# Sliding-window attention and mixture of experts on one core: how a block's values reach the partitions

## The chip, the core and the metric

The kernel runs on one core of a Trainium2 chip. The metric is the device time of one execution in microseconds (us), lower is better. The kernel before takes 676.07 us, the median of three runs (673.82 to 677.14).

## The reference

Eight batches of eight heads with 576 positions of 64 numbers go through masked attention; heads 0 to 3 see the 32 latest keys, heads 4 to 7 see every fourth of the 128 latest. The attention's output, one row of 512 per token (4608 tokens), is then routed over eight experts with a capacity of 576 tokens each, and every expert is a two-layer network.

```python
mask_plain = (rel >= 0) & (rel < window)                                  # window = 32
mask_dil = (rel >= 0) & (rel < window * dilation) & (rel % dilation == 0) # dilation = 4
scores = np.where(masks[None, :, :, :], scores, -1000000000.0)
attn = np.exp(scores - np.max(scores, axis=-1, keepdims=True))
attn = attn / (np.sum(attn, axis=-1, keepdims=True) + 1e-09)
out = np.matmul(attn, v)
...
for e in range(E):
    mask = assigned == e
    out[mask] = np.maximum(x[mask] @ w1[e], 0.0) @ w2[e]
```

## The kernel before, in words

The kernel has two stages: attention (`attention`, L260 to L772), which writes its rows to a scratch tensor `xd` in device memory, and after it the search for the routing and the experts (`moe`). The change touches attention alone.

**Units.** Attention works through 8 batches. A batch has two kinds of heads: kind 0 the plain window, kind 1 the dilated one, whose sequence is put in an order in which it is a plain window of 32 too. A kind of a batch has two units of two heads each, so there are 32 units. For a unit PE makes the masked scores in two forms (`scan`, L498 and L502, for the maxima; `scores`, L509 and L514), ACT takes the exponentials into `E` (L468), PE multiplies them by the values (`values`, L526, tile `px`), DVE divides (L534 to L536, tile `xs`), PE turns the result for the gate (L585), and SP stores `xs` to `xd` (L545): two stores per batch for kind 0 and eight for kind 1.

**The values in SBUF.** `VT[kind][slot]` (tile `v` in the profile) has 128 partitions and nine columns, one for each 64 keys of a sequence; a column holds four heads of 65 numbers (64 and a one). There are two slots per kind, used by even and odd batches. Queries are taken 32 at a time and see 64 keys: even groups of 32 queries see the last 32 keys of the column before and the first 32 of their own, odd groups the first and the last 32 of their own. A column therefore holds, from partition 0 up: 32 keys of the column before, its own first 32, its first 32 again, and its last 32. So each half of a block stands in SBUF twice. The load (`load_v`, L292 to L295) brings all 64 keys to partitions 64 to 127, and copies within SBUF (`shift_v`, L297 to L303) make the other two quarters: L301 moves partitions 96 to 127 to partitions 0 to 31 of the next column, L303 moves partitions 64 to 95 to 32 to 63.

**`load_values`** (L400 to L412) does this once per kind and batch. It issues two loads on SP, columns 0 to 4 and 5 to 8 (325 and 260 KB; rows of 5200 and 4160 bytes). In the first batch DVE and ACT make the copies, in pieces of columns 0 to 4 and 5 to 8. From the second on POOL makes all of them, in pieces of 2, 3, 2 and 2 columns for each of the two quarters, so eight copies per kind and batch, 112 in all. `values` (L526) waits for all loads and copies of its kind and batch (`ready["V", kind, b]`).

**What sets the order.** Nobody writes the order of attention's instructions by hand: each step is an `Op` with an engine, an assumed cost, the steps it depends on and a bonus, and `Schedule.run` (L188) replays them against these costs, takes at each turn the most urgent step that can start, and so writes one order for each engine. A transfer on SP costs 475 ns of SP there, and its landing is assumed from its bytes (`sp`, L336 to L339). Engines then run their orders strictly in turn and wait on semaphores.

**What holds SP back.** `paced` (L321 to L334) adds a wait to a load or store: on a product of PE that the replay found done by then (`K.gate`), or, without one, on an earlier transfer, so that no more than 1.2 MB (`LIMIT`) are under way. The framework also gives every transfer one of eight semaphores in rotation (DMAHW0 to DMAHW7 below). The next transfer that uses a semaphore waits until the one that had it has landed. So no more than eight transfers from SP are under way.

Of the kernel before, what the change touches and what calls it, by code (L numbers as in the profile page):

```python
# [20 lines left out]
B, H, S, D = 8, 8, 576, 64  # L21
# [5 lines left out]
NB = S // 64  # L27
# [18 lines left out]
P_U, B_A, B_K, B_V, B_P, TOL_A, TOL_B, TOL_C, TOL_D = 4680, 15400, -5200, 14500, -105500, 650, 650, 300, 800  # L46
# [213 lines left out]
def attention(tc, ctx, C, load_const, T, xd, Lt, R):  # L260
    nc = tc.nc
# [7 lines left out]
    def op(eng, *a, **k):  # L269
        return K.op(eng, *a, tail=T_E[eng], **k)  # L270
# [6 lines left out]
    VT = [[pk.tile([128, NB, 4, D + 1], F32, name=f"v{x}{s}") for s in range(2)] for x in range(2)]  # L277
# [11 lines left out]
                  for n, k in (("pm", 2), ("pS", 2), ("px", 3)))  # L289
    act = lambda o, i: nc.scalar.activation(o, i, AF.Copy)  # L290

    def load_v(b, kind, c0, c1):  # L292
        w = 4 * (D + 1)
        return nc.sync.dma_start(VT[kind][b % 2][64:, c0:c1].rearrange("p c h d -> p (c h d)"),
                                 T["in_vp" if kind == 0 else "in_vd"][b][:, w * c0:w * c1])  # L295

    def shift_v(b, kind, part, f, c0, c1):  # L297
        t = VT[kind][b % 2].rearrange("p c h d -> p c (h d)")
        if part == 0:
            c1 = min(c1, NB - 1)  # L300
            f(t[:32, c0 + 1:c1 + 1], t[96:, c0:c1])  # L301
        else:
            f(t[32:64, c0:c1], t[64:96, c0:c1])  # L303

    users = {}

    def old(*key):
        u = users.get(key, [])
        users[key] = []
        return u  # L310
# [10 lines left out]
    def paced(fn, bytes_):  # L321

        def run():
            i, under_way = fn().ins, bytes_
            if K.gate:
                return after(i, K.gate, "transfers keep step with the products")
            for prev, z in reversed(flow):
                under_way += z
                if under_way > LIMIT:
                    after(i, prev.name, "few bytes under way")  # L330
                    break
            flow.append((i, bytes_))

        return run  # L334

    def sp(cost, fn, deps, bytes_, b, kind=0):  # L336
        first[0] -= 1e6
        return op("SP", 475 * cost, paced(fn, bytes_) if cost == 1 else fn, deps,
                  B_D - (4 * b + 2 * kind) * P_U if b else first[0], dma=bytes_ / D_R)  # L339
# [4 lines left out]
    ready = {}  # L344
# [55 lines left out]
    def load_values(b, kind):  # L400
        s = b % 2
        oldv = old("v", kind, s)
        ld = {c0: sp(1, lambda c0=c0, c1=c1: load_v(b, kind, c0, c1), oldv, 64 * (c1 - c0) * 4 * 65 * 4, b, kind)
              for c0, c1 in ((0, 5), (5, NB))}
        ready["V", kind, b] = list(ld.values())
        for part in range(2):
            eng = "POOL" if b else ("DVE", "ACT")[part]
            f = {"ACT": act, "DVE": nc.vector.tensor_copy, "POOL": nc.gpsimd.tensor_copy}[eng]
            for c0, c1 in ((0, 2), (2, 5), (5, 7), (7, 9)) if b else ((0, 5), (5, 9)):
                ready["V", kind, b].append(op(eng, {"ACT": 255, "DVE": 190, "POOL": 275}[eng] * (c1 - c0),  # L410
                                              lambda part=part, f=f, c0=c0, c1=c1: shift_v(b, kind, part, f, c0, c1),
                                              [ld[0 if c1 < 6 else 5], ready["b", kind, s]], -4 * b * P_U))  # L412

    load.q = None

# [331 lines left out]
    ready["r"] = sp(1, choosers, (), 131000, 0)  # L747
    load(0, 0, 1)
    load_values(0, 0)
    load(0, 1, 0)  # L750
    const(2)
    load(0, 1, 1)
    load_values(0, 1)
    const(3)

# [5 lines left out]
    for u in range(4 * B):  # L761
        b = u // 4
        if u % 4 == 0 and b:
            for kind in range(2):
                load(b, kind, 0)
                load(b, kind, 1)
                load_values(b, kind)
        Unit(u).build()
# [797 lines left out]
```

## Time and profile before

| what | value |
|---|---|
| median of three runs | 676.07 us (673.82 to 677.14) |
| profiled execution | 676.34 us |
| its span in the profile | 674.4 us |
| attention and its last products | 0 to about 182 us |
| search for the routing, first part | about 182 to 205 us |
| experts | about 205 us to the end |

The span is the stretch from the first to the last instruction in the trace; 1.94 us of the profiled execution's own time lie outside it. Times of the rows below count from the start of the span. PE is the matmul engine and PEld its weight loads, DVE, ACT and POOL are the other compute engines, and SPq rows are transfers as SP issues them.

### The profile page before, as it was taken

The numbers are of one execution on the slowest core, as the hardware profiler recorded it, in microseconds if no ns is written. First come the engines' busy times: TensorE is split into PE (matmuls) and PEld (weight loads), VectorE is DVE, ScalarE is ACT, GpSimd is POOL, SyncE is SP. The second block draws the span as 40 slices with busy tenths as digits, with TensorE's granted clock in tenths as the row PEclk, the third lists the DMA queues.
The fourth block names the chain that finished last, engine by engine and source line by source line (L and its number), as shares of the span: only waits on it lengthen the run. The fifth ranks groups of instructions, "written<-read, shape, count | busy, mean of one in ns | idle before, by whom it ended". The sixth has DMA issues, their size and how long they took to land.

```text
span 674.4 us, 19052 instructions
## 1 busy us (share of the span) xinstructions
PE 629.3 (93%) x7513; PEld 550.1 (82%) x7515; DVE 463.9 (69%) x1576; ACT 294.1 (44%) x644; POOL 208.3 (31%) x316
## 2 busy tenths in 40 slices
PE   7788998889857999999999999999999999999996
PEld 6777887778645988998899799889879978988985
DVE  6577878588677884689799588778959845623310
ACT  5655555355304825855345136334423525424211
POOL 6446754555004317524213112110420311311011
PEclk9999999899957999999999999999999999999999
DMA  8988879784205937967236116314502755213001
GB/s 240 261 255 218 246 219 263 208 227 147 73 1 178 225 70 200 275 142 250 93 97 209 48 56 209 113 55 141 181 33 58 262 181 163 66 37 103 1 24 47
DMA packets 51673, 99.09 MB, mean 147 GB/s; under 512 B 7168, under 2 KB 17152, under 8 KB 51584
## 3 DMA queue, kind: packets, MB, share of 16 engines
q1 hardware_dynamic: 42240, 72.71, 36.2%
q0 software_dynamic: 9344, 25.17, 13.8%
q8 instruction: 59, 0.97, 0.6%
q14 instruction: 30, 0.25, 0.1%
HBM read 72.69 MB, written 18.87 MB: 136 GB/s over the span
## 4 chain that ended last, share of the span: by engine, by line
PE 53%; DVE 19%; issue 14%; DMA 7%; POOL 4%; ACT 1%; POOLq 0%; SPq 0%; DVEq 0%; ACTq 0%
PE py L1432 15%; PE ph L1387 15%; PE px L526 4%; PE pS L514 4%; PE px L585 2%; POOL xg L1336 2%; DVE hb L1408 2%; PE ptx L1350 2%; DMA raw<-in_moe_w 1%; DVE xs L536 1%; DMA v<-in_vd 1%; PE pz L817 1%; POOL out L1458 1%; DVE G L831 1%; PE py L1435 1%
## 5 line engine op out<-in xcount | busy, mean ns | idle before, releaser
L1432 PE MATMUL py<-w2h,hb 128*128 128x512 f32 x512 | 170.4, 398 | 0.0
L1387 PE MATMUL ph<-xh,w1h 128*128 128x256 f32 (+1 forms) x512 | 138.3, 301 | 0.0
L1387 PE MATMUL ph<-xh,w1l 128*128 128x256 f32 (+1 forms) x512 | 136.4, 297 | 0.0
L1387 PE MATMUL ph<-xl,w1h 128*128 128x256 f32 (+1 forms) x512 | 136.2, 296 | 0.0
L1432 PEld LDWEIGHTS py<-w2h,hb 128*128 128x128 f32 x512 | 96.1, 188 | 19.1
L1212 ACT ACTIVATE hb<-ph 128x256 fp32r<-128x256 f32 (+2 forms) x192 | 59.6, 346 | 100.8 <-PE ph L1387 100.6
L1458 POOL DMA_INDIRECT out<-y,idx x40 | 41.8, 1045 | 199.1 <-ACT y L1212 143.5
L1432 PE MATMUL py<-w2l,hb 128*128 128x512 f32 x256 | 99.9, 390 | 0.0
L1387 PEld LDWEIGHTS ph<-xh,w1h 128*128 128x128 f32 x512 | 91.8, 189 | 0.6
L1387 PEld LDWEIGHTS ph<-xl,w1h 128*128 128x128 f32 x512 | 91.6, 190 | 0.0
L1387 PEld LDWEIGHTS ph<-xh,w1l 128*128 128x128 f32 x512 | 91.5, 190 | 0.0
L1408 DVE SCALAR_TENSOR_TENSOR hb<-ph,hb 128x320 fp32r<-128x320 f32 (+1 forms) x128 | 57.1, 453 | 33.4 <-ACT hb L1212 32.4
L468 ACT ACTIVATE E<-pS 128x384 f32<-128x384 f32 x96 | 46.1, 491 | 56.0 <-PE pS L514 53.8
L1212 ACT ACTIVATE y<-py 128x512 f32<-128x512 f32 (+1 forms) x40 | 23.9, 597 | 97.6 <-PE py L1432 78.2
L526 PE MATMUL px<-v,E 128*64 128x65 f32 x1152 | 48.9, 226 | 7.2 <-issue 3.6
L1432 PEld LDWEIGHTS py<-w2l,hb 128*128 128x128 f32 x256 | 48.2, 188 | 8.5
L514 PE MATMUL pS<-q,k 128*64 128x64 f32 x1152 | 53.0, 230 | 0.4 <-issue 0.4
L526 PEld LDWEIGHTS px<-v,E 128*64 128x64 f32 x1152 | 42.7, 139 | 11.8 <-issue 9.9
L1336 POOL DMA_INDIRECT xg<-xd,idx x40 | 41.2, 1030 | 36.2 <-PE ph L1387 26.5
L301 POOL COPY v<-v 32x520 f32<-32x520 f32 (+2 forms) x56 | 33.3, 618 | 53.8 <-DMA v<-in_vp 27.3
L1213 DVE TENSOR_TENSOR xl<-ptx,xh 128x512 fp32r<-128x512 f32 (+1 forms) x36 | 22.9, 636 | 37.5 <-ACT xh L1212 37.4
L1213 DVE TENSOR_TENSOR w2l<-raw,w2h 128x512 fp32r<-128x512 f32 x48 | 31.8, 685 | 21.0 <-ACT w2h L1212 20.3
(203 smaller groups left out, 1136.7 us busy)
## 6 DMA issues: line engine op xcount, KB each, us to landing
raw<-in_moe_w SPq DMA_DIRECT2D x128, 256.0 KB, 4.5
qs<-in_qp SPq DMA_DIRECT2D x16, 288.0 KB, 4.7
k<-in_kp SPq DMA_DIRECT2D x16, 288.0 KB, 3.8
qs<-in_qd SPq DMA_DIRECT2D x16, 288.0 KB, 5.0
k<-in_kd SPq DMA_DIRECT2D x16, 288.0 KB, 4.6
xd<-xs SPq DMA_DIRECT2D x8, 512.0 KB, 5.3
w2l<-raw POOLq DMA_DIRECT2D x16, 256.0 KB, 4.2
v<-in_vp SPq DMA_DIRECT2D x8, 325.0 KB, 6.4
```

What stands on the lines that cost most here:

```text
L301: f(t[:32, c0 + 1:c1 + 1], t[96:, c0:c1])
L468: e = self.op("ACT", 475, lambda j=j, pS=pS: nc.scalar.activation(self.E[:, 3 * j:3 * j + 3].rearrange("p c x -> p (c x)"), pS.tile[:, :38 ...
L514: x = nc.tensor.matmul(pS[64 * h:64 * h + 64, k, :, h], self.K[:, 32 * g:32 * g + 64], self.Q[:, g], start=False, stop=True, skip_group_ch ...
L526: x = nc.tensor.matmul(px[64 * h:64 * h + 64, c - c0, a], self.E[:, k, 64 * a:64 * a + 64], self.V[:, k, 2 * self.ui + a], start=True, sto ...
L585: x = nc.tensor.transpose(pt.tile[:, 128 * (c - c0):128 * (c - c0) + 128], xs[:, c, 2 * ui:2 * ui + 2].rearrange("p a d -> p (a d)"), C["i ...
L1212: act = lambda o, i, f=AF.Copy: nc.scalar.activation(o, i, f)
L1213: sub = lambda e, o, a, b: e.tensor_tensor(o, a, b, op=OP.subtract)
L1336: nc.gpsimd.indirect_dma_start(out=xg[:n], out_offset=None, in_=xd, in_offset=bass.IndirectOffsetOnAxis(ap=box[0][:n, m:m + 1], axis=0))
L1387: nc.tensor.matmul(o, a[:, d * 128:d * 128 + 128], b[:, d, c0:c1], start=((d, i) == pairs[0]), stop=((d, i) == pairs[-1]))
L1408: hl = op("DVE", 335 if j == 0 else 400, lambda: nc.vector.scalar_tensor_tensor(hb[:, CAP + c0:CAP + c1], o, 0.0, hb[:, c0:c1], op0=OP.max ...
L1432: nc.tensor.matmul(py, x, w, start=(f + i == 0), stop=(f == NF - 1 and i == 2))
L1458: s = nc.gpsimd.indirect_dma_start(out=out, out_offset=bass.IndirectOffsetOnAxis(ap=box[0][:n, m:m + 1], axis=0), in_=y[:n], in_offset=None)
```

## The change

The 64 keys of a column are loaded in two transfers instead of one. The first 32 keys go to partitions 32 to 63, the last 32 to partitions 96 to 127, where they are needed too. L301 stays as it is; L303 now copies in the other direction, from partitions 32 to 63 to 64 to 95. A copy depends on the transfer of its own half. The number of copies and the bytes stay as they are; a kind of a batch has four loads instead of two, so attention has 64 loads of values instead of 32. Behind `load_values` every line is numbered one higher than before.

```diff
-    def load_v(b, kind, c0, c1):
-        w = 4 * (D + 1)
-        return nc.sync.dma_start(VT[kind][b % 2][64:, c0:c1].rearrange("p c h d -> p (c h d)"),
-                                 T["in_vp" if kind == 0 else "in_vd"][b][:, w * c0:w * c1])
+    def load_v(b, kind, half, c0, c1):
+        w, p = 4 * (D + 1), 32 + 64 * half
+        return nc.sync.dma_start(VT[kind][b % 2][p:p + 32, c0:c1].rearrange("p c h d -> p (c h d)"),
+                                 T["in_vp" if kind == 0 else "in_vd"][b][32 * half:32 * half + 32, w * c0:w * c1])
...
-            f(t[32:64, c0:c1], t[64:96, c0:c1])
+            f(t[64:96, c0:c1], t[32:64, c0:c1])
...
-        ld = {c0: sp(1, lambda c0=c0, c1=c1: load_v(b, kind, c0, c1), oldv, 64 * (c1 - c0) * 4 * 65 * 4, b, kind)
-              for c0, c1 in ((0, 5), (5, NB))}
+        ld = {(c0, half): sp(1, lambda c0=c0, c1=c1, half=half: load_v(b, kind, half, c0, c1), oldv,
+                             32 * (c1 - c0) * 4 * 65 * 4, b, kind)
+              for c0, c1 in ((0, 5), (5, NB)) for half in range(2)}
...
-                                              [ld[0 if c1 < 6 else 5], ready["b", kind, s]], -4 * b * P_U))
+                                              [ld[0 if c1 < 6 else 5, 1 - part], ready["b", kind, s]], -4 * b * P_U))
```

Since the replay has more steps on SP, it writes other orders for all engines. Three places follow. In the names the part behind the last underscore is a buffer: `v_105` and `v_107` are the slot of odd batches, kind 0 and kind 1.

SP in the sixth batch, from the plain values to the dilated ones; in brackets the semaphores that the transfer waits for. Before:

```order
L294 DMA v_105<-in_vp 64x1300 [waits DMAHW0_49,PE_49,Pool_49]
L294 DMA v_105<-in_vp 64x1040 [waits DMAHW1_49,PE_49,Pool_49]
L545 DMA xd<-xs_124 128x4x256 [waits DMAHW2_49,DVE_49]
L545 DMA xd<-xs_124 64x256 [waits DMAHW3_49,PE_49]
L382 DMA qs_111<-in_qd 128x576 [waits DMAHW4_49,Activation_49]
L382 DMA qs_111<-in_qd 128x576 [waits DMAHW5_49,PE_49]
L384 DMA k_99<-in_kd 128x576 [waits DMAHW6_49,PE_49]
L384 DMA k_99<-in_kd 128x576 [waits DMAHW7_49,PE_49]
L294 DMA v_107<-in_vd 64x1300 [waits DMAHW0_49,PE_49,Pool_49]
L294 DMA v_107<-in_vd 64x1040 [waits DMAHW1_49,PE_49,Pool_49]
```

With the change:

```order
L546 DMA xd<-xs_124 128x4x256 [waits DMAHW0_49,DVE_49,PE_49]
L546 DMA xd<-xs_124 64x256 [waits DMAHW1_49,PE_49]
L382 DMA qs_111<-in_qd 128x576 [waits DMAHW2_49,PE_49,Activation_49]
L382 DMA qs_111<-in_qd 128x576 [waits DMAHW3_49]
L384 DMA k_99<-in_kd 128x576 [waits DMAHW4_49,PE_49]
L384 DMA k_99<-in_kd 128x576 [waits DMAHW5_49,PE_49]
L294 DMA v_107<-in_vd 32x1300 [waits DMAHW6_49,PE_49,Pool_49]
L294 DMA v_107<-in_vd 32x1300 [waits DMAHW7_49,PE_49]
L294 DMA v_107<-in_vd 32x1040 [waits DMAHW0_49,Pool_49]
L294 DMA v_107<-in_vd 32x1040 [waits DMAHW1_49,PE_49]
```

The two loads of `v_107` waited for the two loads of `v_105`, eight transfers back; of the four loads the last two now wait for the stores of `xs_124`, which stand behind all loads of `v_105`.

POOL, the eight copies of `v_107` when they first come up. Before:

```order
L301 COPY v_107<-v_107 32x780 [waits DMAHW0_49]
L303 COPY v_107<-v_107 32x780
L301 COPY v_107<-v_107 32x520
L301 COPY v_107<-v_107 32x520 [waits DMAHW1_49]
L301 COPY v_107<-v_107 32x260
L303 COPY v_107<-v_107 32x520 x3
```

With the change:

```order
L303 COPY v_107<-v_107 32x780 [waits DMAHW6_49]
L301 COPY v_107<-v_107 32x780 [waits DMAHW7_49]
L301 COPY v_107<-v_107 32x520
L301 COPY v_107<-v_107 32x520 [waits DMAHW1_49]
L301 COPY v_107<-v_107 32x260
L303 COPY v_107<-v_107 32x520
L303 COPY v_107<-v_107 32x520 [waits DMAHW0_49]
```

A copy from the first 32 keys now comes first and waits for the first of four transfers alone.

DVE in the first batch, between the maxima of a dilated unit and its chooser rows `R`. Before:

```order
L449 TENSOR_REDUCE mx_118<-pm_140 128x4
L301 COPY v_106<-v_106 32x1300
L301 COPY v_106<-v_106 32x780
L456 CAST R<-pm_140 9x128
L534 TENSOR_SCALAR rec_123<-px_145 128x6
```

With the change:

```order
L450 TENSOR_REDUCE mx_118<-pm_140 128x4
L301 COPY v_106<-v_106 32x1300
L457 CAST R<-pm_140 9x128
L301 COPY v_106<-v_106 32x780
L535 TENSOR_SCALAR rec_123<-px_145 128x6
```

The chooser rows, for which PE's scores wait, now stand ahead of the second copy of values; from here on PE, DVE and ACT have orders of their own.

## Rows read from the trace of the kernel before

**Rows 1.** The page: busy time and share of PE; chain that ended last, by engine.

```profile
PE 629.3 (93%) x7513; PEld 550.1 (82%) x7515; DVE 463.9 (69%) x1576; ACT 294.1 (44%) x644; POOL 208.3 (31%) x316
...
PE 53%; DVE 19%; issue 14%; DMA 7%; POOL 4%; ACT 1%; POOLq 0%; SPq 0%; DVEq 0%; ACTq 0%
```

**Rows 2.** Windows: attention behind its start, and two us behind PE's first long gap.

```profile
core 0: us, PE busy (x) PEld busy (x) DVE busy (x) ACT busy (x) POOL busy (x), PEclk, DMA share, GB/s
17.00:186.00 169.00, 147.59 (x3819) 127.35 (x3817) 123.97 (x416) 87.01 (x192) 83.36 (x133) 0.99 0.76 211
...
50.00:52.00 2.00, 1.71 (x55) 1.62 (x56) 0.98 (x5) 0.00 (x0) 1.92 (x4) 1.00 1.08 358
```

**Rows 3.** Timeline of PE: start us, us, instructions [idle before <- what ended it].

```profile
50.17 0.51 PE L526 MATMUL px<-v,E 128*64 128x65 f32 x9 [1.36 <-issue]
...
112.31 0.28 PE L526 MATMUL px<-v,E 128*64 128x65 f32 x3 [1.16 <-issue]
...
120.35 0.70 PE L526 MATMUL px<-v,E 128*64 128x65 f32 x8 [3.09 <-DMA v<-in_vd]
```

**Rows 4.** Timeline of POOL about the same three places.

```profile
49.29 0.83 POOL L301 COPY v<-v 32x780 f32<-32x780 f32 x1 [4.27 <-DMA v<-in_vp]
...
108.77 0.83 POOL L301 COPY v<-v 32x780 f32<-32x780 f32 x1 [4.59 <-DMA v<-in_vp]
...
110.51 1.53 POOL L301 COPY v<-v 32x520 f32<-32x520 f32 x3
...
119.03 0.83 POOL L301 COPY v<-v 32x780 f32<-32x780 f32 x1 [5.21 <-DMA v<-in_vd]
```

**Rows 5.** Waits of POOL up to 186 us: total us, times, longest us.

```profile
POOL v L301 <- DMA v<-in_vp: 27.3, 6, 5.6
POOL v L301 <- DMA v<-in_vd: 19.3, 6, 5.2
```

**Rows 6.** Timeline of SP's issues: start us, us, transfer and count.

```profile
42.52 1.81 SPq L294 DMA_DIRECT2D v<-in_vp  x2
...
82.11 1.32 SPq L294 DMA_DIRECT2D v<-in_vp  x2
...
101.01 1.24 SPq L294 DMA_DIRECT2D v<-in_vp  x2
...
108.89 2.23 SPq L294 DMA_DIRECT2D v<-in_vd  x2
...
112.71 1.30 SPq L382 DMA_DIRECT2D qs<-in_qp  x2
```

**Rows 7.** Windows: four stretches about the longest gap.

```profile
109.00:111.00 2.00, 2.00 (x55) 1.83 (x54) 1.90 (x8) 1.11 (x3) 1.92 (x3) 1.00 1.05 400
112.00:117.00 5.00, 4.46 (x127) 4.25 (x127) 4.01 (x16) 3.67 (x9) 1.77 (x4) 1.00 1.04 163
...
120.00:122.00 2.00, 1.65 (x31) 1.68 (x33) 0.81 (x3) 0.00 (x0) 1.96 (x4) 0.50 0.38 115
122.00:124.00 2.00, 2.00 (x53) 1.93 (x49) 1.51 (x6) 0.47 (x1) 1.96 (x4) 0.71 0.12 30
```

**Rows 8.** DMA issues, KB each, median us to landing: whole run, then 100 to 118.

```profile
k<-in_kp SPq DMA_DIRECT2D x16, 288.0 KB, 3.8
...
v<-in_vp SPq DMA_DIRECT2D x8, 325.0 KB, 6.4
...
xd<-xs SPq DMA_DIRECT2D x1, 512.0 KB, 7.5
...
v<-in_vd SPq DMA_DIRECT2D x1, 325.0 KB, 10.0
```

**Rows 9.** Line 294: issue time of one load, min/median/max ns, first and last start.

```profile
L294 SPq DMA_DIRECT2D v<-in_vp x16: 471/472/587, 5.4 to 145.8; - x16
```

**Rows 10.** First batch: SP's issue of a table behind values, and PE's wait for it.

```profile
14.74 0.58 SPq L1532 DMA_DIRECT2D const<-in_cf  x1
...
21.44 1.09 PE L585 MATMUL px<-const,xs 128*128 128x128 f32 x8 [2.41 <-DMA const<-in_cf]
```

## The prediction

> **What bounds the kernel now.** I began with the page: PE is busy for 93% of the span and makes 53% of the chain that ended last, DMA 7% [rows 1]. So a transfer counts only where PE stands still for it. The windows then show where that can be: between 17 and 186 us PE is busy for 147.59 of 169 us, so attention has 21.4 us of gaps [rows 2]. The timeline of PE names those that end in the product with the values. Three are long: 1.36 us before 50.17, 1.16 us before 112.31 and 3.09 us before 120.35 [rows 3]. Two are put down to "issue", that is, to nothing that the view can name; the timeline of POOL names it. At 49.29 a copy of values starts after 4.27 us of waiting for its load, it ends at 50.12, and PE goes on at 50.17. At 108.77 the copies start late in the same way, the three of L301 run from 110.51 to 112.04, and PE goes on at 112.31. At 119.03 it happens a third time, after 5.21 us [rows 4]. Together the three gaps are 5.6 us. POOL's own waits for these loads, 46.6 us [rows 5], cost nothing elsewhere, since PE did not stand behind them.
>
> [...] PE had done nearly nothing from 117.3 to 120.3. After the gap of 1.36 us the clock stayed at 1.00 [rows 2]. The clock cost at most 2 x 0.50 + 2 x 0.29 = 1.6 us.
>
> Why are the loads late? With queries, keys and stores alone on the way, 109 to 111 us, DMA moves 400 GB/s at a full share. From 112 to 117 us, with the values on the way, the share is as full and the rate is 163 GB/s [rows 7]. POOL stands 5.21 us for the last of them [rows 4], and one load takes 10.0 us to land [rows 8]. The difference that I see between these transfers is the target: queries and keys go to 128 partitions, values to 64 to 127 alone. [...]
>
> **The change part by part.**
>
> *Rate of the values.* A pair of loads is 325 + 260 KB, 599 kB. At 163 GB/s that is 3.7 us, at 400 GB/s 1.5 us. So a pair gains between 0, if the two halves follow each other and each is as slow as now, and 2.2 us, if they run side by side at full speed. I take the middle, 1.1 us. For more than 0 speaks that queries follow the values from 112.71 on [rows 6] while POOL gets the values only at 119.03: both are on the way together for some five us, from which I infer that the DMA engines are out of step and that two neighbouring short transfers would overlap in part. For less than 2.2 speaks that one queue starts them in order.
>
> *First gap, 1.36 us.* PE waited for the first load of the pair alone. It gains 1.1, and its second half is issued 0.47 us later [rows 9]: -0.6 us.
>
> *Second gap, 1.16 us.* DMA is backed up here and the later issue is hidden; POOL may begin with the first half besides: -1.1 us.
>
> *Third gap, 3.09 us.* Two pairs stand in line, issued at 101.01 and at 108.89 [rows 6], each 1.1 us shorter: -2.2 us. 0.9 us are left, less than the gap after which the clock held: -1.6 us for the clock.
>
> *More issues.* 32 more loads at 0.47 us are 15 us of SP over attention. A batch takes 39.6 / 2 = 19.8 us (42.52 to 82.11, two batches, [rows 6]) and goes from 22 to 26 transfers, some 12 us of SP, so SP itself has room. But at most eight transfers are under way, and the last load of a group now stands behind two more. In the backed-up stretch that costs at least 2 x 0.47 = 0.9 us and, if each must wait for its turn at eight in 7.5 us (the large store, [rows 8]), 2 x 0.94 = 1.9 us. The middle: +1.4 us.
>
> *Copies.* The same eight per kind and batch, the same shapes, only L303 turned round: 0. They are hidden on POOL (31% busy) as long as loads are not late.
>
> *First batch.* PE waits 2.41 us for a table issued behind the values at 14.74 [rows 10]. One pair ahead of it gains 1.1 us; four more issues ahead of it cost up to 1.9 us. Taken as 0, bounds -1.1 and +0.8.
>
> *New order.* The replay gives PE, DVE and ACT other orders. What it can move is the rest of the gaps, 21.4 - 5.6 = 15.8 us. I allow a fifth of it either way, 3 us, and take 0. Bytes, products and the experts stay as they are.
>
> Sum: -0.6 - 1.1 - 2.2 - 1.6 + 1.4 = -4.1 us. From the profiled execution, 676.34 us (span 674.4, 1.94 outside), that gives **672.2 us**. The median of the runs is 0.27 us lower; I leave that inside the range. About 0.5%, 3.4 us, is what a measurement of this kernel can tell from no change.
>
> **The rivals.**
>
> *No difference: the halves follow each other.* Both transfers use the same queue. If a half must be done before the next begins, each is as slow as a pair is now, the 163 GB/s stay, and the three gaps with the clock stay too. What changes then is the later issue, hidden where DMA is full, and the new order: 676.3 us, 673 to 679. For it speaks that the queue is one; against it the five us with two kinds of transfers on the way. [...] The same time comes out if the loads gain but the new order eats it. Chance 0.32.
>
> *Slower: eight transfers are no longer enough.* At eight under way and 19.8 us per batch the mean time to landing may be 8 x 19.8 / 22 = 7.2 us now, and 8 x 19.8 / 26 = 6.1 us with the change. The medians of most transfers are below (3.8 us for keys, 6.4 for values), but in the stretch from 100 to 118 us they reach 7.5 to 10.0 [rows 8]. If the rate of the values does not rise, four more transfers cost 4 x 7.5 / 8 = 3.8 us there: 680.1 us, with one more backed-up batch or an unlucky order 683. SP's orders show the place: the third load of the dilated values now waits for the large store, which stands behind all plain values. Against it: short transfers land sooner, which lifts the limit again. It decides from a mean landing of 6.1 us upwards. Chance 0.20.
>
> *The change does not do what it says.* Both transfers are in SP's order with 32 rows each, so this has no chance of its own.
>
> **How the numbers follow.** The forecast has 0.48: gaps shrink by 3 to 7 us, and its own range is 667.5 to 674. Nearly all of that, 0.43, lies more than 3.4 us below; 0.05 goes to "same". The first rival gives 0.32, of which 0.01 falls on either side, hence 0.30 for "same" and 0.01 each for faster and slower. The second gives 0.20, of which 0.18 is slower by over 3.4 us and 0.02 is not. Faster 0.44, same 0.37, slower 0.19. At full relief all of 1.36 + 1.16 + 3.09 + 1.6 = 7.2 us would go, 669.1 without the later issue, less 1.1 for the table and more or less 3 for the order; I put the lower end at 667.5. The upper end is the second rival's 680. Below lies about 1 in 12, above about the same.
>
> **What would show it.** Right: values land after about 5 us instead of 6.4 and after 8 or less in the sixth batch; the DMA rate with values on the way is well over 163 GB/s; the gaps before L526 add up to less than 2 us; the clock keeps 1.00 from 110 to 130 us. Landing times as before with the same three gaps speak for the first rival. Waits of SP's L294 and L546 for a landing, a few us in sum, and gaps that move elsewhere speak for the second. The prediction is wrong if the values' rate doubles and the time still stays, for then the new order would weigh more than the gaps, or if PE's gaps before L526 go and others of the same size open at DVE or ACT.

## The result, and the profile after

The changed kernel takes 678.12 us (median of 20 runs, 673.84 to 683.41). The kernel before, timed on the same chip between its runs, takes 673.11 us (20 runs, 669.08 to 680.65). The ratio is 1.0062 [1.0041, 1.0082]: **slower by 0.6%**, some 4 us, where 0.6% faster was forecast. The time lies inside the range, the sign is wrong. The profiled execution of the changed kernel took 678.58 us.

The page first, in the lines that answer to [rows 1]: PE's busy time and the chain by engine are nearly what they were.

```profile
PE 630.5 (93%) x7513; PEld 549.1 (81%) x7515; DVE 468.4 (69%) x1576; ACT 295.4 (44%) x644; POOL 209.6 (31%) x316
...
PE 52%; DVE 20%; issue 14%; DMA 7%; POOL 4%; ACT 2%; POOLq 0%; SPq 0%; DVEq 0%; ACTq 0%
```

What the change was to do to the transfers, it did. POOL's waits for values (total us, times, longest us; before 27.3 and 19.3, [rows 5]):

```profile
POOL v L303 <- DMA v<-in_vp: 14.5, 4, 4.4
POOL v L303 <- DMA v<-in_vd: 13.5, 5, 4.5
```

They fell from 46.6 to 28.0 us. How large the fall is depends on the execution: the second profile of the kernel before, shown further down, has 37.4 us, so that 9.2 of these 18.6 us are no more than two executions of one kernel differ by. The next rows are firmer. The time to landing of all loads of tile `v`, first in the kernel before, then in the changed one, where a load is half as large:

```profile
DMA to landing us min/median/max: 4.3/6.1/10.0
```

```profile
DMA to landing us min/median/max: 2.3/4.4/6.3
```

And the queue that carries all of SP's transfers, from 0 to 170 us (packets, MB, share of 16 engines), before and after: the same bytes take 73.4% of the DMA engines' time instead of 80.2%.

```profile
q1 hardware_dynamic: 22496, 37.96, 80.2%
```

```profile
q1 hardware_dynamic: 23006, 37.96, 73.4%
```

Where, then, did the time go? PE's waits from 17 to 190 us name a transfer that is none of the values: the wait for the identity table of [rows 10], at that time 2.41 us, is now the longest in attention. PE's timeline in the first batch shows what stands around it. Before:

```profile
16.41 0.61 PE L526 MATMUL px<-v,E 128*64 128x65 f32 x11
16.89 0.28 PE L509 MATMUL pS<-R,const 73*64 73x64 bf16 x6
16.98 0.57 PE L514 MATMUL pS<-q,k 128*64 128x64 f32 x12
17.36 0.33 PE L498 MATMUL pm<-const,const 128*64 128x320 bf16 x2
...
18.46 0.57 PE L514 MATMUL pS<-q,k 128*64 128x64 f32 x12
```

After:

```profile
16.45 0.34 PE L527 MATMUL px<-v,E 128*64 128x65 f32 x3
20.72 0.55 PE L586 MATMUL px<-const,xs 128*128 128x128 f32 x3 [3.93 <-DMA const<-in_cf]
21.20 0.33 PE L499 MATMUL pm<-const,const 128*64 128x320 bf16 x2
...
22.43 0.89 PE L515 MATMUL pS<-q,k 128*64 128x64 f32 x12
```

The table did not come later. It arrived 0.7 us earlier, by 20.72 instead of 21.44 us. But PE came to it 2.2 us sooner: in the new order the first unit's products for the gate (L586) stand ahead of scans and scores which before were done first, and PE keeps its order. It stood still for 3.93 us with that work behind it. Then the clock fell:

```profile
0.00:20.00 20.00, 13.33 (x258) 9.90 (x259) 12.96 (x39) 9.19 (x13) 10.03 (x28) 1.00 0.82 239
20.00:40.00 20.00, 18.24 (x445) 15.83 (x445) 11.71 (x37) 12.69 (x26) 7.20 (x11) 0.91 0.77 227
...
22.00:24.00 2.00, 2.00 (x36) 1.88 (x33) 1.38 (x3) 2.00 (x2) 0.00 (x0) 0.55 0.71 164
24.00:26.00 2.00, 2.00 (x35) 1.67 (x35) 0.68 (x2) 1.52 (x6) 1.62 (x3) 0.60 0.74 195
```

The granted clock is the third number from the end of a line (columns as in [rows 2]). At 0.55 and 0.60 these four us did at most 2 x 0.45 + 2 x 0.40 = 1.7 us less work than at full clock. In its first 20 us PE was busy for 13.33 us. In the kernel before it was busy for 15.34, and the wait of 2.41 us left the clock at 1.00:

```profile
0.00:20.00 20.00, 15.34 (x334) 12.18 (x335) 14.40 (x42) 10.68 (x15) 10.65 (x28) 1.00 0.87 237
20.00:40.00 20.00, 17.00 (x448) 14.54 (x450) 12.08 (x39) 11.55 (x25) 10.00 (x16) 1.00 0.85 247
```

### The profile page after: what moved, and what is told of

It is laid out like the page before. It is cut to its first block, busy times and chain, and to the rows that moved or that the text cites. A ratio compares the mean times of both kernels' runs of the same rounds, so it can differ in the third digit from the quotient of the medians.

```text
span 676.7 us, 19129 instructions
## 1 busy us (share of the span) xinstructions
PE 630.5 (93%) x7513; PEld 549.1 (81%) x7515; DVE 468.4 (69%) x1576; ACT 295.4 (44%) x644; POOL 209.6 (31%) x316
## 4 chain that ended last, share of the span: by engine, by line
PE 52%; DVE 20%; issue 14%; DMA 7%; POOL 4%; ACT 2%; POOLq 0%; SPq 0%; DVEq 0%; ACTq 0%
PE py L1433 15%; PE ph L1388 15%; PE pS L515 4%; PE px L527 3%; PE px L586 2%; POOL xg L1337 2%; DVE xs L537 2%; DVE hb L1409 2%; PE ptx L1351 2%; DMA raw<-in_moe_w 2%; PE pz L818 1%; POOL out L1459 1%; DVE G L832 1%; PE py L1436 1%; PE py L1438 1%
## 5 line engine op out<-in xcount | busy, mean ns | idle before, releaser
L303 POOL COPY v<-v 32x520 f32<-32x520 f32 (+1 forms) x56 | 36.9, 684 | 41.2 <-DMA v<-in_vp 14.5
```

What stands on the lines that cost most here:

```text
L303: f(t[64:96, c0:c1], t[32:64, c0:c1])
```

## The experiments

Each ratio is to the kernel before, timed on the same chip in the same series; the median of the kernel before is given beside each. Runs with the same such median are one series; the series ran on different chips, so a difference between ratios of two series is less firm than one within a series. "Old order" is the order that the replay writes for the kernel before, "new order" the one of the changed kernel.

### Transfers and order, one without the other

**Old order, two loads.** The replay sees one load, as before, and so writes the order of before; the load issues two transfers, one to each half.

```diff
-        return nc.sync.dma_start(VT[kind][b % 2][64:, c0:c1]...)
+        return [nc.sync.dma_start(VT[kind][b % 2][p:p + 32, c0:c1]..., T[...][b][r:r + 32, ...])
+                for r, p in ((0, 32), (32, 96))]
...
-            f(t[32:64, c0:c1], t[64:96, c0:c1])
+            f(t[64:96, c0:c1], t[32:64, c0:c1])
```

> The order of PE, DVE, ACT and POOL is that of the kernel before, to the instruction; only SP issues each load of values as two loads of 32 partitions. Theory A (the new order costs the time; two loads by themselves are a gain): 1 to 3 us below the kernel before, so about 0.997 of it; loads of values land in under 5 us, and PE's gaps before the product with the values add up to under 2.5 us. Theory B (more and shorter transfers cost the time: their issue and the limit of eight under way): as slow as the change, 1.004 to 1.008 of the kernel before, and SP's waits for landings grow by 3 us or more.

0.9974 [0.9947, 1.0002]; 672.58 us against 673.37.

**New order, one load.** The mirror image: the replay plans four loads per kind and batch and so writes the order of the change; the first half's step issues the whole load to 64 to 127, the second half's step issues nothing. (In the limit of 1.2 MB under way such a load counts with half its bytes.)

```diff
-        w, p = 4 * (D + 1), 32 + 64 * half
-        return nc.sync.dma_start(VT[kind][b % 2][p:p + 32, c0:c1]...)
+        if half:
+            return None
+        return nc.sync.dma_start(VT[kind][b % 2][64:, c0:c1]...)
...
-            f(t[64:96, c0:c1], t[32:64, c0:c1])
+            f(t[32:64, c0:c1], t[64:96, c0:c1])
```

> The order of PE, DVE, ACT and POOL is that of the change, to the instruction; SP issues one load of 64 partitions to 64 to 127, as before. Theory A: as slow as the change or slower, since the order stays and the loads land later again: 1.006 to 1.012 of the kernel before. Theory B: within 0.3% of the kernel before.

1.0131 [1.0097, 1.0166]; 682.02 us against 673.37. The two runs part the change in two. The order alone costs 1.3%, 8.8 us by ratio (0.0131 x 673.37). The transfers alone give 0.3% with the old order (the interval just takes in no gain) and 0.7% with the new one (1.0131 to 1.0062, whose intervals do not meet). The table is waited for in this kernel too:

```profile
20.86 0.90 PE L591 MATMUL px<-const,xs 128*128 128x128 f32 x3 [3.73 <-DMA const<-in_cf]
```

With the old order and two loads the same products wait 0.89 us, and the clock is 1.00 from 20 to 40 us:

```profile
20.24 1.09 PE L588 MATMUL px<-const,xs 128*128 128x128 f32 x8 [0.89 <-DMA const<-in_cf]
```

**Old order, two loads into the same half.** Is it the halves, or just that the transfers are smaller? The loads go to 64 to 95 and 96 to 127. The edit against the run with the old order and two loads:

```diff
-                for r, p in ((0, 32), (32, 96))]
+                for r, p in ((0, 64), (32, 96))]
...
-            f(t[64:96, c0:c1], t[32:64, c0:c1])
+            f(t[32:64, c0:c1], t[64:96, c0:c1])
```

> The order of all compute engines is that of the kernel before; each load of values is two loads of 32 partitions, to 64 to 95 and to 96 to 127, so within the old target. Theory P (the target partitions make the loads fast or slow): landing stays as long as before, 5.5 us or more in the median, the DMA share up to 170 us stays above that of the first run, and the time is 0.998 to 1.006 of the kernel before. Theory S (shorter transfers alone make them fast, the target does not matter): landing and time as in the first run (0.997).

1.0042 [1.0004, 1.0079]; 681.63 us against 678.30. The queue's line from 0 to 170 us, first for the loads to both halves, then for the same number of loads to one half:

```profile
q1 hardware_dynamic: 23616, 38.55, 74.4%
```

```profile
q1 hardware_dynamic: 23008, 37.96, 80.7%
```

Loads to both halves need a smaller share of the DMA engines although more of the kernel's bytes fell into the 170 us; a split within one half leaves the share where it was (80.2% before). It takes 0.4% longer than the kernel before; the 32 extra transfers are the likely reason, which no run shows by itself. Ten profiles bear out the shares: the four with loads to one half have 77.9 to 80.7%, the six with loads to both have 73.4 to 74.6%. Among the four is the second profile of the kernel before, with the same 38.55 MB as the run with loads to both halves:

```profile
q1 hardware_dynamic: 23099, 38.55, 79.6%
```

So what eases the queue here is the target: 74.4% with loads to 32 to 63 and 96 to 127, 80.7% with as many to 64 to 95 and 96 to 127. Why the target matters is not shown.

### The table in the first batch

**The change, table early.** The identity table alone (one of the three transfers of L1533) is issued ahead of the first batch's dilated values. The replay is not told, so all other orders stay.

```diff
     def load_v(b, kind, half, c0, c1):
         w, p = 4 * (D + 1), 32 + 64 * half
+        if (b, kind, half, c0) == (0, 1, 0, 0):
+            load_const(4)
...
-        for t, src in parts[i:i + 1] if i < 3 else parts[3:]:
+        for t, src in parts[i:i + 1] if i < 3 else parts[3:4] if i == 4 else parts[4:]:
```

> The change with one transfer moved: the identity table, 64 KB, is issued ahead of the first batch's dilated values instead of behind them; all compute engines keep their order. Theory A, in the form that the new order lets PE run into the table (gap of 3.93 us at 16.8, then the lower clock): the gap falls below 1 us, the clock stays at 1.00 from 20 to 40 us, and the time falls by 4 to 5 us, to 0.999 to 1.001 of the kernel before. If the loss is spread over the order instead, the gap goes too but the time falls by 2 us or less, to 1.003 or more. Theory B: 1.003 or more as well.

1.0033 [1.0008, 1.0058]; 675.82 us against 673.37. PE now waits 0.22 us at these products, and the clock in the same stretch is 1.00:

```profile
16.97 0.55 PE L588 MATMUL px<-const,xs 128*128 128x128 f32 x3 [0.22 <-DMA const<-in_cf]
```

```profile
22.00:24.00 2.00, 2.00 (x78) 2.00 (x75) 0.47 (x3) 1.50 (x5) 1.71 (x3) 1.00 0.84 226
24.00:26.00 2.00, 2.00 (x56) 1.92 (x52) 1.43 (x6) 1.63 (x3) 0.69 (x1) 1.00 0.64 192
```

The wait is nearly gone. The ratio falls by 0.3%, a third of what the order costs with two loads (1.0062 - 0.9974 = 0.9%), but the two intervals overlap, so this size is loose. In the profiled executions the first batch's last exponentials end at 29.7 us in the change and at 26.0 with the table early, 3.7 us sooner. The rest of the loss is elsewhere.

**Before, table early.** The same edit in the kernel before.

> The kernel before with the same transfer moved, the control to the run with the change. PE's gap of 2.41 us at 19.0 shrinks to under 0.5 us. Theory A: 1 to 2.5 us faster than the kernel before (0.996 to 0.9985), so clearly less than what the change gains by the same move. If it gains 4 us too, the table is not what separates the two kernels.

0.9988 [0.9958, 1.0018]; 672.66 us against 673.37. There a wait of 1.5 to 2.4 us without a fall of the clock goes, and no gain can be told from none.

**Old order, two loads, table early.** The two edits that helped, together.

> The first run (old order, two loads to 32 to 63 and 96 to 127) with the identity table ahead of the first batch's dilated values. If the gains add: 0.994 to 0.997 of the kernel before. In the first run PE's gap at the table was 0.89 us, so at most 0.9 us more than there.

0.9955 [0.9924, 0.9986]; 675.37 us against 678.30. This is the lowest ratio measured, 0.4% under the kernel before and about 1% under the changed one; the intervals do not tell it from those of 0.9964 to 0.9979 elsewhere among the experiments.

### Which part of the plan does it

**New plan in the first batch alone.** Every load is two transfers, but only in the first batch does the replay see four loads per kind.

```diff
+        two = b == 0
...
+              for c0, c1 in ((0, 5), (5, NB)) for hs in (((0,), (1,)) if two else ((0, 1),))}
```

> Two loads for every batch; the planner sees four loads per kind in the first batch only, so PE's order begins as in the change. Theory A, head: the product for the gate runs into the table again (gap of 3 us or more before 22 us, then the lower clock), and the time is 1.002 to 1.008 of the kernel before. Theory A, tail alone: the head costs nothing by the end, and the time depends on where the last unit's values stand in PE's order.

1.0045 [1.0014, 1.0076]; 680.37 us against 678.30. PE waits 4.13 us for the table, as in the changed kernel.

**New plan from the second batch on.** `two = b > 0`.

> Two loads for every batch; the planner sees four loads per kind from the second batch on, so PE's order begins as in the kernel before. No gap of over 1.5 us before 22 us and no lower clock there. Theory A: 3 to 5 us of the loss of the new order are gone; 0.996 to 1.003 of the kernel before, the lower end if the last unit's values are not behind the gate's products, the upper end if they are.

0.9967 [0.9934, 1.0000]; 675.93 us against 678.30. The wait for the table is 1.39 us. So it is not the four loads of every batch that cost: the two extra loads per kind ahead of the first products turn the replay onto another path. But the replay carries a different start through all later batches, so the pair does not tell whether the loss sits in the first batch or behind it.

**Another order by way of another cost.** Is the old order a lucky one? In the kernel before, the replay's cost of an SP issue goes from 475 to 550 ns; the first batch's order on PE keeps its form.

```diff
-        return op("SP", 475 * cost, ...
+        return op("SP", 550 * cost, ...
```

> The kernel before, transfers as before, with the planner's cost of one issue of SP set from 475 to 550 ns. The order of PE begins as in the kernel before (three score groups of the second dilated unit ahead of the first product for the gate) and differs later. Theory H (the first batch's order is what costs): 0.997 to 1.004 of the kernel before, with no gap over 3 us before 22 us. Rival (any other order than the tuned one is worse by about as much): 1.006 to 1.013.

1.0057 [1.0025, 1.0089]; 676.58 us against 673.55. There is no long wait for the table (0.98 us), and the time is as bad as the change's.

**And by another rate.** The replay's DMA rate goes from 262 to 250, which draws the gate's products forward in the first batch as the change does.

```diff
-RAW1, D_R, NQ, AHEAD_W = 8, 262, (2, 2), (3, 4)
+RAW1, D_R, NQ, AHEAD_W = 8, 250, (2, 2), (3, 4)
```

> The kernel before, transfers as before, with the planner's rate of DMA set from 262 to 250 bytes per ns. Its order puts two products for the gate of the first batch early, as the change does. Theory H: PE runs into the identity table, a gap of over 3 us before 22 us and the lower clock behind it, and 1.004 to 1.013 of the kernel before. Rival: no more than the run with the planner's issue cost.

1.0105 [1.0061, 1.0149]; 681.26 us against 673.55. PE waits for the table, 2.79 us where over 3 were expected, and the clock is 0.91 from 20 to 40 us, as in the changed kernel:

```profile
20.66 0.76 PE L585 MATMUL px<-const,xs 128*128 128x128 f32 x5 [2.79 <-DMA const<-in_cf]
```

Two small changes of the plan's numbers, with no transfer altered, cost 0.6 and 1.1%. Together with the change's own that makes three orders beside the old one, all slower with one load of 64 partitions: the old order is a good one among those tried, and an edit that disturbs it has that to lose. Not every other order is worse: the one that plans four loads from the second batch on has 0.9967 with two transfers per load, the old order 0.9974.

### Where the rest of the order's loss sits

The profiles pointed at the end of attention. Windows from 17 us to the seventh batch's last exponentials, and from there to the start of the search, for the changed kernel and for the old order with two loads:

```profile
17.00:155.10 138.10, 122.63 (x3241) 106.19 (x3241) 106.73 (x332) 74.42 (x162) 79.96 (x125) 0.99 0.79 242
155.10:189.80 34.70, 27.27 (x613) 21.98 (x614) 23.70 (x92) 12.69 (x30) 5.45 (x9) 0.95 0.22 68
```

```profile
17.00:150.60 133.60, 121.49 (x3293) 106.09 (x3289) 105.86 (x344) 75.94 (x165) 79.28 (x125) 1.00 0.83 253
150.60:180.10 29.50, 25.29 (x571) 20.79 (x568) 20.77 (x79) 11.16 (x29) 5.20 (x8) 0.94 0.23 68
```

In the second stretch PE stands still for 34.70 - 27.27 = 7.4 us with the new order and for 4.2 us with the old, and DVE has 13 instructions more to do. These are single executions; the old order with two loads and the table early stands still for 32.40 - 27.18 = 5.2 us there:

```profile
148.70:181.10 32.40, 27.18 (x584) 22.66 (x584) 19.87 (x79) 11.11 (x29) 5.21 (x8) 0.91 0.21 63
```

Four runs tested whether that is the loss, or where else it sits.

**Table early, and the last unit's values ahead of the gate's products.** The bonus of the last batch's gate work in the replay goes from 3000 to 0 in the version "change, table early".

```diff
-NS, B_E, DIRECT = (2, 2), 3000, 7
+NS, B_E, DIRECT = (2, 2), 0, 7
```

> The change with the table early (third run) and one of the planner's bonuses for the last batch set from 3000 to 0. The order is the same up to the last batch; there PE makes the last unit's products with the values ahead of the gate's products of the unit before it. Theory T (the place of the last values in the order costs what the tail of attention is longer by): from the last exponentials to the start of the search the stretch falls by 1.5 to 2 us, and the time is 0.9995 to 1.002 of the kernel before. Rival: PE has the same products to make in either order, and the time stays at 1.002 to 1.005.

1.0015 [0.9992, 1.0038]; 674.38 us against 673.55. From 1.0033 this is no difference that the intervals can tell, and the standstill behind the seventh batch's exponentials stayed 7.3 us (33.80 less 26.53). The values came earlier, but the products behind them then waited for DVE. The ratio lies where the theory put it, but the stretch shrank only from 34.20 to 33.80 us and not by 1.5 to 2, so this part of the tail's order is not shown to be a cause.

**Spliced orders.** The last three kernels all have two loads to both halves and the early table. Their engines follow one order up to a point and the other from there on: the numbers of attention's steps are written out in a table, and the replay takes at each turn the first of them that can be placed.

```diff
-    def run(self, idle):
+    def run(self, idle, rank=None):
...
+            if rank:
+                for x in sorted(sum(ready.values(), []), key=lambda x: rank[x.n]):
+                    p = self.place(x) if x.buf else (0.0, 0)
+                    if p is not None:
+                        best = (max(free.get(x.eng, 0.0), x.ready, p[0], self.next if x.dma else 0.0), x)
+                        break
...
-    K.run(idle)
+    K.run(idle, {n: i for i, n in enumerate(ORDER)})
```

New order up to the seventh batch's last exponentials, then the old:

> Base: two loads to both halves, identity table ahead of the dilated values. The order of the change is followed up to the last exponentials of the seventh batch, and what is left then follows the order of before. Theory 'end' (the new order loses at the end of attention, where PE stands still for 7.2 to 7.4 us in the stretch behind those exponentials against 4.1 with the order of before): the end shrinks by some 3 to 4 us, ratio about 0.997 to 0.999. Rival 'spread' (the loss is everywhere, or lies in the work that is left over at that point and not in its order): the stretch behind those exponentials stays 33 us or longer and the ratio stays near the 1.0033 of the change with the table early.

1.0020 [0.9998, 1.0042]; 674.64 us against 673.14.

Old order up to there, then the new:

> The mirror image: the order of before up to the last exponentials of the seventh batch, and what is left then in the order of the change. Theory 'end': the end alone costs 3 to 4 us, ratio about 1.001 to 1.003, and PE stands still for 7 us in the stretch behind those exponentials. Rival 'spread': ratio as with the order of before throughout, 0.9955 to 0.997, and about 4 us of standstill there.

0.9979 [0.9955, 1.0003]; 670.82 us against 673.14.

New order up to the first batch's last exponentials, then the old:

> The order of the change up to the last exponentials of the first batch alone, then the order of before; two loads to both halves, identity table ahead of the dilated values. Theory 'table' (in the first batch the new order costs nothing but PE's run into the missing identity table): with the table early the ratio is that of the order of before, 0.9955 to 0.998. Rival: the new order of the first batch costs also by its leftovers, then 1.001 or more.

0.9964 [0.9944, 0.9984]; 671.35 us against 673.14. Put in a row, all with two loads, these ratios take the order apart; only the third and the fourth are of one series:

| what follows the new order | ratio |
|---|---|
| everything, table late (the change) | 1.0062 [1.0041, 1.0082] |
| everything, table early | 1.0033 [1.0008, 1.0058] |
| all but the end | 1.0020 [0.9998, 1.0042] |
| the first batch alone | 0.9964 [0.9944, 0.9984] |
| nothing | 0.9955 [0.9924, 0.9986] |

The table is 0.3%, with intervals that overlap. The end is 0.1% here and 0.2% in the mirror image (0.9979 against 0.9955), less than the intervals can tell from nothing, so the theory "end" fell in the main. The first batch's order costs nothing that the intervals can tell once the table is there. The largest step, 0.6% or 3.8 us, comes with the order that is followed between the first batch's and the seventh batch's last exponentials, and it is the only step whose two intervals do not meet. What this order leaves over for the end counts with it: behind those exponentials PE has 611 instructions in the one run and 569 in the other. In the two profiled executions the seventh batch's last exponentials lie 2.7 us apart (156.0 and 153.3 us), the start of the search 4.0 (187.6 and 183.6). The profiles don't resolve it further. In the windows above PE's gaps up to the seventh batch's exponentials are 138.10 - 122.63 = 15.5 us with the new order and 133.60 - 121.49 = 12.1 with the old, and 3.93 - 0.89 = 3.0 us of that difference is the table's; behind those exponentials the two mirror images stand still for 4.9 us (new order, old end: 31.60 less 26.71) and 5.8 us (old order, new end: 32.10 less 26.31), so that the standstill follows the end's order only in part. One execution of a kernel differs from the next by as much as is sought here: the kernel before reaches those exponentials at 157.4 us in its first profile and at 153.3 in its second. What in the order of the second to seventh batch costs 3.8 us stays open.

### The kernel before, once more

A second profile of the unchanged kernel, for the three gaps on which the forecast stood.

> The kernel before, unchanged, for a second profile. If the gap of 3.09 us before 120.35 and the lower clock behind it belong to the kernel, they come again and the profiled time is about the same as in the first profile. If they were chance of that one execution, which lay 3 us above the median of the 20 executions timed with the result, they are gone, the search starts 4 us or more earlier than at 187.6 us, and the forecast counted 3.8 us that a usual execution does not lose.

670.88 us in one execution, span 669.0, 5.4 us less than the profile that the prediction read. PE's first product with the values at the third place, and the windows of [rows 7] again:

```profile
121.42 0.97 PE L526 MATMUL px<-v,E 128*64 128x65 f32 x25
```

```profile
112.00:117.00 5.00, 4.67 (x127) 3.94 (x122) 4.72 (x15) 4.01 (x9) 2.31 (x4) 1.00 0.94 252
...
120.00:122.00 2.00, 1.62 (x35) 1.26 (x34) 1.44 (x6) 1.23 (x4) 1.90 (x4) 1.00 0.45 92
122.00:124.00 2.00, 2.00 (x52) 1.24 (x48) 1.40 (x6) 0.98 (x3) 1.08 (x2) 1.00 1.01 309
```

The gap of 3.09 us, the clock of 0.50 and the 163 GB/s are not there. The first gap is (1.21 us before 50.32), the second is not.

## Why the prediction was wrong, point by point

**"I allow a fifth of it either way, 3 us, and take 0" (new order).** This is the step that failed. The order alone cost 8.8 us with one load and, by 1.0062 - 0.9974, 5.9 us with two. The prediction said itself that the forecast falls if "the new order would weigh more than the gaps", but priced an order by a share of the gaps that the old one left. An order is not bounded by those: it can open gaps that were closed, and this one did. PE's gaps up to the seventh batch's last exponentials are 15.5 us in the changed kernel and 12.1 with the old order and two loads. Some of the loss is PE's early call for the table; most of it, by the ratios, comes with the order of the second to seventh batch, and what in that order costs it stays open.

**"First batch. Taken as 0, bounds -1.1 and +0.8."** The term asked when the table would land, and landing moved by 0.7 us to the good side, within its bounds. It did not ask when PE would get to the table. The replay's product for the gate does not list the table among what it depends on, so the order could call it with nothing to hold it back but the transfer itself: 3.93 us and the clock instead of 2.41. Undoing it gave 0.3%, about 2.0 us, with intervals that overlap.

**Third gap -2.2 and its clock -1.6.** 3.8 of the forecast's 4.1 us stood on a place that one execution had and the next had not. The 1.6 us are worked out from the 0.50 and 0.71 of [rows 7]; in the second profile the clock is 1.00 in both stretches. The profiled execution (676.34 us) was also 3.2 us above the median of 673.11 that the kernel before then had beside the change. In the second profile PE's waits before L526 that are put down to "issue", as the first two were, come to 3.8 us (6 times), in the changed kernel to 2.6 (3 times): some 1.2 us were to be had.

**Rate of the values, 1.1 us per pair.** Right in kind. Loads land after 4.4 us (some 5 were forecast), with the values on the way DMA moves 303 GB/s (112 to 118 us), and with the old order the time falls by 0.26%, 1.8 us, near the low side and with an interval that just takes in no gain. That is transfers and issues together. Against the split within one half, which has the same issues, the two halves give 1.0042 - 0.9974 = 0.7%, 4.6 us, an estimate, since the two runs are of different series. That it lies near the 5.5 us that the terms for the gaps and the clock add up to is luck: 3.8 of these stood on the third gap of one execution. The 163 GB/s from which the term was worked out were one execution's; the second profile has 252 in the same five us.

**More issues, +1.4.** An issue was cheaper than taken: one of a half load took 365 ns (plain) or 371 ns (dilated) as the median, not 472. The extra transfers as a whole were not. The split within one half has the extra transfers without the other target, and it took 0.42% more than the kernel before, 2.8 us, with an interval from 0.3 to 5.3 us that takes in 1.4. Where these us arise is not shown. They do not show as waits for the limit of eight: in the changed kernel the waits of L294 and L546 for a landing, the sign that the prediction named, come to 2.0 us up to 200 us, in the kernel before to 5.7.

**Copies, 0.** Right: POOL is busy for 209.6 us against 208.3.

**The rivals.** "The halves follow each other" is out: the same split gives 74.4% of the DMA engines' time to both halves and 80.7% to one. The prediction saw the difference between fast and slow transfers in the target, and that the target counts, these shares show. "Eight transfers are no longer enough" named nearly the time that came, 680.1 us, and for another reason: its condition, a mean landing of 6.1 us or more, was not met. For the values the median was 4.4 and the longest landing 6.3, and no kind of transfer has a median above 5.2 up to 186 us. That the time falls into a rival's range does not make the rival right. What came was a term of the sum. Both rivals name it in passing, the first as "the new order eats it", the second as "an unlucky order", and neither has it cost more than the allowed 3 us.

## What to carry to other kernels

Where a planner writes the order, an edit of the transfers is two edits: hold the order fixed to learn what the transfers are worth, then decide about the order by itself. Two runs, the new transfers in the old order and the old transfers in the new order, would have told at once that the order costs the time, though not which part of it. A gap of a few us in one profile is worth a second profile of the same kernel before a forecast rests on it, and a wait is priced by when its engine gets there as much as by when the data land.

## What was not expected of the hardware

Sending the same bytes to partitions 32 to 63 and 96 to 127 instead of 64 to 127 took the queue's share of the DMA engines from 80.2% to 74.4% with the same order of instructions, with twice as many loads and a little more data in the stretch (38.55 MB instead of 37.96); 64 to 95 and 96 to 127 did not (80.7%). Over the ten profiles the shares do not overlap: 73.4 to 74.6% with loads to both halves, 77.9 to 80.7% with loads to one.

The clock fell to 0.55 (22 to 24 us, changed kernel) after PE had stood still for 3.93 us. In the run with the new order of the first batch alone a wait of 3.15 us for keys did the same (PE's timeline, then its window, columns as above):

```profile
47.28 0.32 PE L571 MATMUL pm<-k,q 128*64 128x64 bf16 x9 [3.15 <-DMA k<-in_kp]
```

```profile
48.00:52.00 4.00, 4.00 (x66) 3.60 (x62) 2.52 (x10) 1.77 (x4) 1.22 (x2) 0.59 0.83 252
```

After the wait of 0.89 us for the table (old order, two loads) it did not fall, nor after the 2.41 us of the kernel before: it was 1.00 from 20 to 40 us in both. In the run "before, table early" eleven products took 0.88 us at 16.30 and, at another place, 0.54 us:

```profile
16.30 0.88 PE L516 MATMUL pS<-q,k 128*64 128x64 f32 x11
...
17.87 0.54 PE L516 MATMUL pS<-q,k 128*64 128x64 f32 x11
```

In the changed kernel twelve such products took 0.89 us at 22.43, where the clock was 0.55. So I take it to have been low there too, an estimate, with no wait for the table ahead of it: a long wait for the table is not the only thing that goes before a low clock. The kernel with the wait of 3.15 us is still one of the fastest by its median: the longest gap of one execution says little of the rest.
